# Sink-window attention with a squared-ReLU expert layer: shorter first legs for chunks 0 and 1, and another order of their attention

## The chip, the cores and the metric

One Trainium2 chip, one of its cores. The metric is the device time of one execution in microseconds. The engines of the core are TensorE (PE; its weight loads are listed as PEld), VectorE (DVE), ScalarE (ACT), GpSimd (POOL) and SyncE (SP), which issues nearly all DMAs. Each engine runs its instructions in the order in which they stand, and waits where the next one lacks its data.

## What is computed

```python
# q, k, v: (4, 8, 768, 64); n_sink 4, window 128
scores = q @ k.T / 8
keep = is_sink | in_window          # the first 4 keys, and the 128 keys up to the query
a = softmax(where(keep, scores, -1e9))      # sums get 1e-9 added
x = (a @ v)                         # heads side by side: (3072, 512)
h = maximum(x @ w_in, 0)            # w_in (512, 2048)
out = (h * h) @ w_out               # w_out (2048, 512)
```

## The kernel before

The 3072 rows of x are worked in eight chunks of 384 rows (two for each batch). A chunk has four pairs of heads and three blocks of 128 queries. Attention of one pair goes through these steps: `score` (TensorE multiplies q by the keys of the block, VectorE masks and finds the row's maximum, ScalarE takes the exponential and its sum); `normalise` (VectorE's reciprocals, then GpSimd scales the probabilities P, three pieces for each head, and copies the sink columns to PSK); `probs` (TensorE transposes P, ScalarE or VectorE copies the result to PTF); `sink_keys` (the same for the sink columns); and `values` (TensorE multiplies by v into xo, ScalarE writes the upper part of x, VectorE the rest, xl). For chunks 0 and 1 `probs` and `sink_keys` stand together in `tail`, a generator of three steps.

The expert layer runs over 16 blocks of 128 hidden columns. For one block TensorE does twelve matmuls of 384 columns (ph, from x and w_in), ScalarE takes the ReLU r and its square gh, VectorE the rest of the square gl, and then TensorE adds nine matmuls of 512 columns into three accumulators po (from gh, gl and w_out). A block is four steps of the generator `moe`, here called quarter steps. The matmuls use fp32r in two parts, upper and rest, so each weight row is split into two parts first.

The weights come as 32 rows of 512 KB: four of w_in and four of w_out for each quarter of the hidden columns, in this order. `split_steps` splits one row in five steps on VectorE (lines 561 to 574) and two copies on ScalarE (lines 560 and 573). The tile m between them has a single buffer. A row is loaded when the one two places ahead of it has been split.

A leg is a chunk's pass over a part of the hidden blocks. Where a chunk has more than one leg, `evacuate` stores the accumulators po to DRAM (part), and the next leg's `evacuate` loads them and VectorE adds them (line 518). Chunks 0 and 1 go in legs of one half, chunk 0, 1, 0, 1, so that their first legs need only half of the rows. The other six chunks have one leg each.

Up to the end of chunk 1's attention the order on all engines is written out by hand (`tc.manual_schedule`): the loop from line 653 on runs chunk 0's attention and the scores of chunk 1's first pair (pair 4), and `fill(n)` puts n steps of row splitting between. Then the list `todo` has the rest of chunk 1's attention in small items, and after every quarter step of chunk 0's first leg some steps of splitting and one item of `todo` follow. QUANTA is the number of these quarter steps, EARLY the number of rows split by then. Behind that, a plan (line 757) gives for each leg up to which of the attention units of later chunks it goes (`ready[1]` is 0, `ready[2]` the end of chunk 2's units), between which rows it splits, and how fast; the scheduler orders the engines by priority there.

Scores in `todo` go into two banks (tag att), and so do the transposed probabilities; in the loop ahead of it scores also use the banks h, o0 and o1, which the expert layer needs later. Ahead of that, matmuls on zeros (`busy`) fill TensorE while the first pair is prepared.

Of the kernel before, what the change touches and what calls it, by code (L numbers as in the profile page):

```python
# [8 lines left out]
F32 = mybir.dt.float32  # L9
# [9 lines left out]
P = 128  # L19
# [22 lines left out]
def sink_window_attention_moe(  # L42
# [25 lines left out]
    with ExitStack() as fast:  # L68
# [206 lines left out]
        def normalise(c, p, heads):  # L275
# [10 lines left out]
            for hh in heads:  # L286
                Pt = st["P"][hh]
                j0 = 1 if half == 0 else 0
                if c > 1:

                    nc.gpsimd.tensor_tensor(  # L291
                        Pt[:, j0:NQ, 0:P], Pt[:, j0:NQ, 0:P], Pt[:, j0:NQ, BS:BAND], op=ALU.add
                    )
                for j in range(NQ):
                    n = P if j < j0 else (BS if c > 1 else BAND)
                    nc.gpsimd.tensor_scalar(  # L296
                        Pt[:, j, 0:n], Pt[:, j, 0:n], rs[:, hh, j : j + 1], 1.0, op0=ALU.mult, op1=ALU.mult
                    )
                own = slice(hh * NS, hh * NS + NS)
                src = Pt[:, i0:NQ, P:BS]  # L300
                to = PSK[p % 2 if c < 2 else 0].rearrange("p q (t c) -> p q t c", c=2 * NS)[:, 0 : NQ - i0]
                nc.gpsimd.tensor_copy(to[:, :, 0:3:2, own], src.unsqueeze(2).broadcast_to([P, NQ - i0, 2, NS]))
                nc.gpsimd.tensor_tensor(to[:, :, 1, own], src, f32(to[:, :, 0, own]), op=ALU.subtract)
# [201 lines left out]

        def evacuate(c, f0, f1, po):
            for t in range(NQ):
                pool, tag = (ap3, "PTF") if c == NCHUNK - 1 and t == 2 else (mp, "ob")
                ob = pool.tile([P, DM], F32, tag=tag, name=f"ob_{c}_{f0}_{t}")
                r0 = c * TOK + t * P  # L510
                if c == NCHUNK - 1 and t == NQ - 1:
# [9 lines left out]
                else:  # L521
                    nc.vector.tensor_copy(ob, po[t])  # L522
                if f1 < NFC:
                    part[c, t] = dp.tile([P, DM], F32, tag=f"part{c}{t}", name=f"part_{c}_{t}")
                    nc.sync.dma_start(out=part[c, t], in_=ob)
                else:
                    nc.sync.dma_start(out=out[r0 : r0 + P, :], in_=ob)
# [77 lines left out]
                split.append(n)  # L605
                yield

        FH = NFC // 2
        legs = [(0, 0, FH), (1, 0, FH), (0, FH, NFC), (1, FH, NFC)] + [(c, 0, NFC) for c in range(2, NCHUNK)]
        products = moe(legs)  # L610
        QUANTA = 4 * FH
        EARLY = HALF + 2
        with tc.manual_schedule(engines={E.PE, E.DVE, E.Activation, E.Pool, E.SP}):
            steps = row_steps()

# [34 lines left out]
            split_sinks = load_sinks(0)  # L650
            busy(7)

            for s in range(NPAIR + 1):
                if s > 0:
                    load_qk(*pairs[s + 1])
                for i, tags in enumerate((("att", "att"), ("h", "h"), ("o0", "o1"))):
                    scores(s, i, tags)
                    fill(1)
                fill(1)

                normalise(*pairs[s], (0, 1))
# [5 lines left out]
                if s > 0:  # L667
# [5 lines left out]
                    if rest:  # L673
                        rest()
                    next(t)
                    fill(1)
                    next(t)
                else:
                    fill(1)
            rest = values(*pairs[NPAIR - 1], True)  # L680
            fill(2)
            rest()

            todo = []
            for s in range(NPAIR + 1, 2 * NPAIR + 1):
                if s < 2 * NPAIR:
                    todo += [lambda s=s: (s + 1 < 2 * NPAIR and load_qk(*pairs[s + 1]), scores(s, 0))]
# [10 lines left out]
            todo.append(lambda: values(*pairs[2 * NPAIR - 1]))  # L698
            for n in range(QUANTA):
                next(products)  # L700
                fill(2 if n < QUANTA // 2 and n % 3 or n % 4 == 0 or n >= QUANTA - 12 else 1)
                if todo:
                    todo.pop(0)()
            while len(split) < EARLY:
# [49 lines left out]

        LEAD = 2.5

        plan = [(ready[1], EARLY, 27, 1.0), (ready[1] + 24, 27, NROW, 0.7), (ready[2], NROW, NROW, 1.0)]
        plan += [(ready[min(c + 1, NCHUNK - 1)], NROW, NROW, 1.0) for c in range(2, NCHUNK)]
        flag = None
        checked = 0  # L760
# [219 lines left out]
```

## Time and profile before

| | us |
|---|---|
| median of three runs | 709.92 (709.29 to 710.59) |
| the profiled execution | 708.76 |
| its span, first to last instruction | 706.7 |
| TensorE busy | 687.6 |
| VectorE busy | 437.6 |
| ScalarE busy | 428.7 |
| GpSimd busy | 230.2 |

The busy times are of the whole span. Matmuls are pipelined, so the duration of one overlaps with the next; the distance from start to start is the shorter time.

### The profile page before, as it was taken

To read this page: it belongs to the slowest core of one execution; us is meant where nothing else is said; L and a number is where in the kernel's file an instruction comes from. 1 tells how busy PE (TensorE), PEld (TensorE's weight loads), DVE (VectorE), ACT (ScalarE), POOL (GpSimd) and SP (SyncE) were. 2 spreads that over 40 slices of the span, in tenths; PEclk is the share of its full clock that TensorE was granted. 3 is DMA by queue.
4 is the path that set the end of the run, shared out by engine and by line. 5 is a ranking of instruction groups with operands and counts; after the bars stand their busy time and mean duration, and the time that the engine had idled before them with its cause. 6 is when DMAs were issued, how large, how long until landed. Compare 5 with 4: busy or idle time off the path is not lost.

```text
span 706.7 us, 11716 instructions
## 1 busy us (share of the span) xinstructions
PE 687.6 (97%) x3866; PEld 593.9 (84%) x3866; DVE 437.6 (62%) x1183; ACT 428.7 (61%) x1200; POOL 230.2 (33%) x436
## 2 busy tenths in 40 slices
PE   8789999999999999999999999999999999999996
PEld 4557788998888888888888888889888898889995
DVE  8998889945657655565656565665555655542231
ACT  5887777755666766766676676667767454422221
POOL 6645400043455424323433443332344233200000
PEclk9999999999999999999999999999999999999998
DMA  8475457421534433333343532344333310000001
GB/s 262 144 233 169 129 163 233 142 74 42 149 65 120 131 107 94 85 108 107 94 112 104 150 90 80 95 128 115 98 88 84 96 44 15 1 11 36 1 0 50
DMA packets 37028, 71.51 MB, mean 101 GB/s; under 512 B 4384, under 2 KB 14368, under 8 KB 36960
## 3 DMA queue, kind: packets, MB, share of 16 engines
q1 hardware_dynamic: 36816, 70.55, 34.1%
q8 instruction: 33, 0.54, 0.3%
q14 instruction: 35, 0.29, 0.1%
q10 hardware_dynamic: 144, 0.13, 0.1%
HBM read 62.80 MB, written 7.86 MB: 100 GB/s over the span
## 4 chain that ended last, share of the span: by engine, by line
PE 86%; ACT 5%; DVE 3%; DMA 3%; issue 1%; SPq 0%; ACTq 0%; DVEq 0%
PE po L494 35%; PE ph L457 35%; PE xo L398 6%; PE s L264 4%; PE pt L368 2%; ACT P L271 2%; PE xo L401 2%; DMA kn<-in_k_dram 1%; PE s L260 1%; PE pt L350 1%; ACT m L560 1%; DVE P L268 1%; DMA part<-ob 1%; PE pss L310 1%; DMA raw<-in_moe_w_in_dram 1%
## 5 line engine op out<-in xcount | busy, mean ns | idle before, releaser
L457 PE MATMUL ph<-x,wi 128*128 128x384 f32 x1536 | 305.8, 340 | 0.0
L457 PEld LDWEIGHTS ph<-x,wi 128*128 128x128 f32 x1536 | 265.0, 188 | 8.8 <-issue 1.4
L494 PE MATMUL po<-wo,gh 128*128 128x512 f32 (+1 forms) x770 | 244.3, 398 | 1.1 <-DVE ob L522 0.6
L232 POOL TENSOR_TENSOR KS<-kn,KS 128x408 fp32r<-128x408 f32 (+1 forms) x48 | 58.5, 1218 | 318.9 <-ACT KS L231 315.1
L494 PEld LDWEIGHTS po<-wo,gh 128*128 128x128 f32 x770 | 135.8, 188 | 19.9 <-issue 1.4
L494 PE MATMUL po<-wo,gl 128*128 128x512 f32 x385 | 151.6, 394 | 0.0
L271 ACT ACTIVATE P<-P,nbs 128x264 f32<-128x264 f32 (+1 forms) x192 | 94.4, 492 | 75.5 <-DVE nbs L268 75.1
L465 ACT ACTIVATE r<-ph 128x384 f32<-128x384 f32 x128 | 62.3, 486 | 91.8 <-PE ph L457 89.2
L475 DVE TENSOR_TENSOR ph<-ph,r 128x384 f32<-128x384 f32 x104 | 58.4, 562 | 72.6 <-ACT r L465 72.5
L268 DVE CUSTOM_DVE_ANT_0 P<-s,masks 128x264 f32<-128x264 f32 x160 | 67.1, 429 | 57.2 <-PE s L264 53.8
L296 POOL TENSOR_SCALAR P<-P,rs 128x136 f32<-128x136 f32 (+2 forms) x192 | 85.4, 460 | 34.6 <-DVE rs L285 17.8
L494 PEld LDWEIGHTS po<-wo,gl 128*128 128x128 f32 x385 | 72.2, 188 | 16.0
L479 DVE TENSOR_TENSOR gl<-ph,gh 128x384 fp32r<-128x384 f32 x128 | 71.1, 556 | 23.3 <-ACT ph L472 12.8
L468 ACT ACTIVATE gh<-r 128x384 fp32r<-128x384 f32 x128 | 67.2, 525 | 3.0
L234 DVE TENSOR_TENSOR QS<-qn,QS 64x384 fp32r<-64x384 f32 x48 | 47.3, 984 | 26.5 <-ACT QS L233 26.1
L291 POOL TENSOR_TENSOR P<-P 128x256 f32<-128x256 f32 (+1 forms) x48 | 50.4, 1050 | 24.1 <-ACT P L271 23.6
L264 PE MATMUL s<-KS,QS 128*128 128x264 f32 (+1 forms) x288 | 57.4, 281 | 0.3 <-DVE nbs L268 0.3
L264 PEld LDWEIGHTS s<-KS,QS 128*128 128x128 f32 x288 | 52.0, 188 | 5.6 <-DVE nbs L268 1.2
L374 DVE TENSOR_TENSOR PTF<-pt,halves 128x256 f32<-128x256 f32 x96 | 36.3, 419 | 22.3 <-PE pt L368 21.7
L398 PE MATMUL xo<-PTF,vn 128*64 128x256 f32 (+1 forms) x448 | 47.4, 348 | 2.5 <-ACT PTF L357 2.5
L398 PEld LDWEIGHTS xo<-PTF,vn 128*64 128x64 f32 x448 | 31.7, 138 | 19.8 <-issue 10.1
L231 ACT CAST KS<-kn 128x408 fp32r<-128x408 f32 (+1 forms) x48 | 28.2, 588 | 32.5 <-issue 18.9
(104 smaller groups left out, 632.4 us busy)
## 6 DMA issues: line engine op xcount, KB each, us to landing
raw<-in_moe_w_in_dram SPq DMA_DIRECT2D x16, 512.0 KB, 4.5
raw<-in_moe_w_out_dram SPq DMA_DIRECT2D x16, 512.0 KB, 3.5
half<-in_moe_w_in_dram SPq DMA_DIRECT2D x32, 256.0 KB, 3.2
half<-in_moe_w_out_dram SPq DMA_DIRECT2D x32, 256.0 KB, 3.0
kn<-in_k_dram SPq DMA_DIRECT2D x24, 272.0 KB, 4.2
qn<-in_q_dram SPq DMA_DIRECT2D x32, 192.0 KB, 3.7
out_dram<-ob SPq DMA_DIRECT2D x23, 256.0 KB, 2.3
kn<-in_k_dram SPq DMA_DIRECT2D x24, 204.0 KB, 3.6
```

Of the source, the lines that this page charges most:

```text
L232: nc.gpsimd.tensor_tensor(KS[:, 1, 0:nk], st["kn"][:, hh, 0:nk], f32(KS[:, 0, 0:nk]), op=ALU.subtract)
L264: nc.tensor.matmul(ps[:, 0:n], st["QS", hh][:, qcols], flat[:, a, c0 : c0 + n], start=(a == 0), stop=(a == 1))
L268: nc.vector.tensor_tensor_reduce(Pt[:, i, 0:n], ps[:, 0:n], mask[:, 0:n], -SCALE, BIG, ALU.add, ALU.min, nb)
L271: nc.scalar.activation(Pt[:, i, 0:n], Pt[:, i, 0:n], AF.Exp, bias=nb, scale=-1.0, accum_out=sm[:, i : i + 1])
L296: nc.gpsimd.tensor_scalar(Pt[:, j, 0:n], Pt[:, j, 0:n], rs[:, hh, j : j + 1], 1.0, op0=ALU.mult, op1=ALU.mult)
L398: nc.tensor.matmul(xo[h * D : h * D + D, cols], lhsT, rhs, start=(n == 0), stop=False, skip_group_check=True)
L457: nc.tensor.matmul(ph[:, 0:TOK], wi_at(i, cc, fc), xt[:, cc, :], start=(m == 0), stop=(m == 3 * NCC - 1),)
L465: nc.scalar.activation(r, ph[:, 0:TOK], AF.Relu)
L468: nc.scalar.activation(gh, r, AF.Square)
L475: nc.vector.tensor_tensor(ph[:, 0:TOK], ph[:, 0:TOK], r, op=ALU.mult)
L479: late = lambda: nc.vector.tensor_tensor(gl, ph[:, 0:TOK], f32(gh), op=ALU.subtract)
L494: nc.tensor.matmul(po[t][:, e], gt[:, ts_], wo[f][:, i, e], start=(f == f0 and j == 0), stop=(f == f1 - 1 and j == 2), skip_group_check=True,)
```

## The change

There are now three cuts of the hidden blocks for chunks 0 and 1: a quarter, a quarter and a half, chunk 0 and 1 in turn, so six legs instead of four. The first leg has 16 quarter steps instead of 32, EARLY is 9 rows instead of 18, and after each quarter step an item of `todo` comes ahead of the splitting steps (one or two of them) and another behind. In chunk 0's loop most splitting steps between scores go away, except for pair 0. Of pair 4's three groups of scores only the first stands ahead of chunk 0's last values; the other two are the first items of `todo`. Pair 3's second head is scaled by ScalarE instead of GpSimd. The sums of the second quarter leg use the three PTF buffers instead of the two ob buffers, and line 470's `spare` (not changed) now holds for the four blocks of chunk 0's second quarter, whose squares go to ScalarE.

```diff
@@ normalise
                     n = P if j < j0 else (BS if c > 1 else BAND)
+                    if (c, p, hh) == (0, NPAIR - 1, 1):
+                        nc.scalar.activation(Pt[:, j, 0:n], Pt[:, j, 0:n], AF.Copy, scale=rs[:, hh, j : j + 1])
+                        continue
                     nc.gpsimd.tensor_scalar(
@@ evacuate
-                pool, tag = (ap3, "PTF") if c == NCHUNK - 1 and t == 2 else (mp, "ob")
+                pool, tag = (ap3, "PTF") if c == NCHUNK - 1 and t == 2 or f0 == NFC // 4 else (mp, "ob")
...
-        FH = NFC // 2
-        legs = [(0, 0, FH), (1, 0, FH), (0, FH, NFC), (1, FH, NFC)] + [(c, 0, NFC) for c in range(2, NCHUNK)]
+        FQ, FH = NFC // 4, NFC // 2
+        cuts = ((0, FQ), (FQ, FH), (FH, NFC))
+        legs = [(c, f0, f1) for f0, f1 in cuts for c in range(2)] + [(c, 0, NFC) for c in range(2, NCHUNK)]
         products = moe(legs)
-        QUANTA = 4 * FH
-        EARLY = HALF + 2
+        QUANTA = 4 * FQ
+        EARLY = NCC + 5
...
-            for s in range(NPAIR + 1):
+            for s in range(NPAIR):
                 if s > 0:
                     load_qk(*pairs[s + 1])
+                ahead = s == 0
                 for i, tags in enumerate((("att", "att"), ("h", "h"), ("o0", "o1"))):
                     scores(s, i, tags)
-                    fill(1)
+                    if ahead or i == NQ - 1:
+                        fill(1)
                 fill(1)
...
                     next(t)
-                    fill(1)
                     next(t)
                 else:
                     fill(1)
+            load_qk(*pairs[NPAIR + 1])
+            scores(NPAIR, 0)
+            fill(1)
+            rest = values(*pairs[NPAIR - 2], True)
+            load_v(*pairs[NPAIR])
+            t = tail(NPAIR - 1, ("o2", "h"))
+            next(t)
+            fill(1)
+            rest()
+            next(t)
+            fill(2)
+            next(t)
+            fill(1)
             rest = values(*pairs[NPAIR - 1], True)
-            fill(2)
+            fill(3)
             rest()
-            todo = []
+            todo = [lambda i=i: scores(NPAIR, i) for i in range(1, NQ)] + [lambda: normalise(*pairs[NPAIR], (0, 1))]
...
                 next(products)
-                fill(2 if n < QUANTA // 2 and n % 3 or n % 4 == 0 or n >= QUANTA - 12 else 1)
+                if todo:
+                    todo.pop(0)()
+                fill(1 + n % 2)
                 if todo:
                     todo.pop(0)()
...
-        plan = [(ready[1], EARLY, 27, 1.0), (ready[1] + 24, 27, NROW, 0.7), (ready[2], NROW, NROW, 1.0)]
+        plan = [(ready[1], EARLY, 14, 1.0), (ready[1], 14, 18, 1.0), (ready[1], 18, 23, 1.0)]
+        plan += [(ready[1] + 10, 23, NROW, 0.8), (ready[2], NROW, NROW, 1.0)]
```

In the rows that follow, a name ends with the number of its buffer; s and P carry pair and head ahead of it (s also the block of queries), ph the hidden block, po the first block of its leg and the accumulator. The chunk is not printed.

On VectorE, the scores of pair 2, before:

```order
L268 ISA P_2_1_362,nbs<-s_2_1_0_363,mask_117 128x128
L268 ISA nbs 128x1
L563 SCALAR_TENSOR_TENSOR t_2_339<-raw_177,t_2_339 128x512
L268 ISA P_2_0_357,nbs<-s_2_0_1_368,masks 128x264
L268 ISA nbs 128x1
L268 ISA P_2_1_362,nbs<-s_2_1_1_372,masks 128x264
L268 ISA nbs 128x1
L565 TENSOR_SCALAR m_340<-raw_177 128x512
L268 ISA P_2_0_357,nbs<-s_2_0_2_377,masks 128x264
```

and now:

```order
L268 ISA P_2_1_352,nbs<-s_2_1_0_353,mask_117 128x128
L268 ISA nbs 128x1
L268 ISA P_2_0_347,nbs<-s_2_0_1_357,masks 128x264
L268 ISA nbs 128x1
L268 ISA P_2_1_352,nbs<-s_2_1_1_361,masks 128x264
L268 ISA nbs 128x1
L268 ISA P_2_0_347,nbs<-s_2_0_2_365,masks 128x264
```

The steps of row 2 between the three groups are gone; the row is split later.

On TensorE, from chunk 0's last transposes to the first matmuls of the expert layer, before, all three score groups of pair 4 stand ahead of pair 2's and pair 3's values:

```order
L260 MATMUL s_0_0_0_546<-kn_0_447,qn_0_446 128x264
L260 MATMUL s_0_1_0_551<-kn_0_447,qn_0_446 128x264
L260 MATMUL s_0_0_1_556<-kn_0_447,qn_0_446 128x264
L260 MATMUL s_0_1_1_560<-kn_0_447,qn_0_446 128x264
L260 MATMUL s_0_0_2_569<-kn_0_447,qn_0_446 128x264
L260 MATMUL s_0_1_2_573<-kn_0_447,qn_0_446 128x264
L398 MATMUL xo_2_596<-PTF_2_2_537,vn_2_414 64x256
```

and now, the first group alone:

```order
L353 MATMUL pt_2_2_509<-ident,P_2_1_352 128x128 x4
L260 MATMUL s_0_0_0_523<-kn_0_434,qn_0_433 128x264
L260 MATMUL s_0_1_0_528<-kn_0_434,qn_0_433 128x264
L401 MATMUL xo_2_536<-PTF_2_2_514,vn_2_402 64x256
L401 MATMUL xo_2_536<-PTF_2_1_507,vn_2_402 64x128
```

Four of the six score rows have moved behind chunk 0's last values and the first matmuls of ph_0.

On TensorE, the stretch in which pair 5 (pair 1 of chunk 1) begins, now:

```order
L460 MATMUL ph_0_599<-x_0_400,wi 128x384
L260 MATMUL s_1_0_0_660<-kn_1_517,qn_1_516 128x264
L260 MATMUL s_1_1_0_665<-kn_1_517,qn_1_516 128x264
L260 MATMUL s_1_0_1_670<-kn_1_517,qn_1_516 128x264
L260 MATMUL s_1_1_1_674<-kn_1_517,qn_1_516 128x264
L260 MATMUL s_1_0_2_683<-kn_1_517,qn_1_516 128x264
L260 MATMUL s_1_1_2_687<-kn_1_517,qn_1_516 128x264
L353 MATMUL pt_0_0_707<-ident,P_0_0_522 128x128 x4
L460 MATMUL ph_1_714<-x_0_399,wi 128x384 x2
```

where before it stood like this:

```order
L260 MATMUL s_1_1_0_674<-kn_1_540,qn_1_539 128x264
L457 MATMUL ph_0_653<-x_0_411,wi 128x384 x2
L457 MATMUL ph_0_653<-x_0_412,wi 128x384
L457 MATMUL ph_0_653<-x_0_411,wi 128x384 x2
L457 MATMUL ph_0_653<-x_0_412,wi 128x384
L260 MATMUL s_1_0_1_695<-kn_1_540,qn_1_539 128x264
```

Half a block of the expert layer stood between pair 5's first two groups of scores, and stands there no more.

## Rows read from the trace of the kernel before

**Rows 1.** The page: the span, and TensorE's busy time, share and instructions.
```profile
span 706.7 us, 11716 instructions
...
PE 687.6 (97%) x3866; PEld 593.9 (84%) x3866; DVE 437.6 (62%) x1183; ACT 428.7 (61%) x1200; POOL 230.2 (33%) x436
```

**Rows 2.** Stretches: length; PE, PEld, DVE, ACT, POOL busy; granted clock; DMA share; GB/s.
```profile
17.20:24.60 7.40, 6.10 (x37) 4.46 (x36) 6.75 (x26) 5.80 (x18) 4.84 (x11) 0.77 0.24 77
...
31.60:41.10 9.50, 7.02 (x50) 4.60 (x51) 9.05 (x31) 6.09 (x18) 5.79 (x15) 1.00 0.72 238
41.10:61.10 20.00, 19.03 (x99) 13.60 (x98) 18.34 (x55) 17.21 (x46) 8.45 (x14) 1.00 0.57 186
...
103.60:134.30 30.70, 30.07 (x151) 26.92 (x150) 29.35 (x66) 24.36 (x46) 0.00 (x0) 1.00 0.60 193
```

**Rows 3.** Waits of TensorE, 11 to 41 us: total, times, longest.
```profile
PE s L260 <- ACT PTF L357: 3.7, 3, 1.8
PE xo L398 <- ACT PTF L357: 2.5, 1, 2.5
```

**Rows 4.** TensorE in order of time: start, duration, instruction, idle before it.
```profile
18.93 1.38 PE L260 MATMUL s<-kn,qn 64*128 64x128 f32 x10 [1.30 <-ACT PTF L357]
20.24 2.27 PE L398 MATMUL xo<-PTF,vn 128*64 128x256 f32 x12
...
25.72 1.38 PE L260 MATMUL s<-kn,qn 64*128 64x128 f32 x10 [0.62 <-ACT PTF L357]
27.03 1.30 PE L398 MATMUL xo<-PTF,vn 128*64 128x256 f32 x12
...
31.60 2.21 PE L260 MATMUL s<-kn,qn 64*128 64x264 f32 x12 [1.76 <-ACT PTF L357]
...
39.04 1.88 PE L398 MATMUL xo<-PTF,vn 128*64 128x256 f32 x12 [2.48 <-ACT PTF L357]
...
41.08 1.21 PE L457 MATMUL ph<-x,wi 128*128 128x384 f32 x6
...
96.27 0.44 PE L401 MATMUL xo<-SK,VS 128*128 128x384 f32 x1
```

**Rows 5.** VectorE in order of time, one step and the same place five later.
```profile
125.12 0.69 DVE L563 SCALAR_TENSOR_TENSOR t<-raw,t 128x512 int32<-128x512 int32 x1
...
127.34 0.55 DVE L479 TENSOR_TENSOR gl<-ph,gh 128x384 fp32r<-128x384 f32 x1
```

**Rows 6.** Groups by line, 0 to 110 us: busy, mean ns, idle before.
```profile
L271 ACT ACTIVATE P<-P,nbs 128x264 f32<-128x264 f32 x40 | 20.2, 506 | 5.3 <-DVE nbs L268 5.1
...
L560 ACT COPY m<-raw 128x512 uint16<-128x512 uint16 x22 | 17.0, 772 | 3.1 <-issue 1.4 <-DVE wi L574 1.1 <-DVE wo L574 0.4
```

**Rows 7.** GpSimd in order of time, the first and the last instruction of pair 4.
```profile
37.67 1.40 POOL L296 TENSOR_SCALAR P<-P,rs 128x264 f32<-128x264 f32 x3 [3.26 <-DVE rs L285]
...
42.29 0.75 POOL L303 TENSOR_TENSOR PSK<-P,PSK 128x24 fp32r<-128x24 f32 x1
```

**Rows 8.** TensorE in order of time, a score group of chunk 1.
```profile
42.21 0.72 PE L260 MATMUL s<-kn,qn 64*128 64x264 f32 x4
```

**Rows 9.** The chain that ended last, around 115 us: start, us, what.
```profile
114.83 2.08 PE ph L457 x12
116.91 2.06 PE po L494 x9
```

**Rows 10.** VectorE and TensorE in order of time, at two ends of legs.
```profile
109.28 0.69 DVE L522 COPY ob<-po 128x512 f32<-128x512 f32 x1 [1.11 <-DMA part<-ob]
...
110.03 0.73 PE L494 MATMUL po<-wo,gh 128*128 128x512 f32 x2 [0.63 <-DVE ob L522]
...
182.85 0.73 PE L494 MATMUL po<-wo,gh 128*128 128x512 f32 x2 [0.47 <-DVE ob L518]
```

**Rows 11.** Stretches, as in rows 2.
```profile
21.00:22.00 1.00, 1.00 (x8) 0.62 (x5) 1.00 (x6) 1.00 (x4) 0.63 (x2) 0.50 0.00 0
...
36.00:40.00 4.00, 1.52 (x13) 0.89 (x12) 3.59 (x13) 2.99 (x9) 2.18 (x6) 1.00 0.99 326
```

## What I predict

> **What bounds the kernel now.** I read the page first: TensorE is busy for 687.6 of 706.7 us [rows 1]. So only three things can shorten the kernel: TensorE standing still, TensorE at the lower clock, or TensorE running pieces slowly. The end of the program, the last leg and its stores, is not touched. The stretch table then shows where the stops are [rows 2]: from 31.6 to 41.1 us TensorE works 7.02 of 9.50 us, while VectorE works 9.05. From 103.6 to 134.3 us VectorE works 29.35 of 30.70 us, yet TensorE only stops for 0.63. The waits of TensorE between 11 and 41 us name ScalarE's copy of the transposed probabilities, 3.7 us before scores and 2.5 us before values [rows 3]. In order of time these are the stops before 18.93, 25.72, 31.60 and 39.04 us, and the first matmul of the expert layer starts at 41.08 us [rows 4]. That copy is late because ScalarE and VectorE run in order, and between two attention steps each does a step of a weight row.
>
> **The change, part by part.** Everything is counted as TensorE time lost or won.
>
> *Fewer row steps ahead of the first expert matmul.* Before, 31 steps of weight splitting stand ahead of it (5 for pair 0, then four times 6, then 2); after, 22 (5, then three times 3, then 8). Five VectorE steps of one row take 125.12 to 127.34 us, so 0.44 us each from start to start [rows 5]. Pairs 1 to 3 lose three steps each, 1.3 us of VectorE, and 0.6 of a row's two ScalarE operations, the one of 772 ns [rows 6] and one somewhat shorter. I walked the new order from 11.4 us on, up to where it equals the old one, with the durations of these rows. Scores of pair 2 resume at 17.8 instead of 18.93 us, since the copy no longer stands behind row work; pair 3's at 23.6 instead of 25.72; pair 4's at 29.1 instead of 31.60.
>
> *The second head of pair 3 on ScalarE.* GpSimd ends a later pair 5.4 us after its start (37.67 to 43.04) [rows 7]. The trace has no such scaling on ScalarE. Its nearest row is the exponential with the same shape, 506 ns [rows 6]; three take 1.3 us from start to start if they need no accumulator read. They run beside GpSimd's first head, and hold ScalarE's next copies for that long. Bounds: from a loss of 1.3 us, if those copies are what is waited for, to a gain of 1.4 us, if GpSimd is. In my walk both end within 0.5 us of each other, so I count a gain of 0.4 us, already in the times below.
>
> *Values before scores.* With two of pair 4's three score groups moved behind, values of pair 3 start at 34.1 instead of 39.04 us and the first expert matmul at 35.6 instead of 41.08 us [rows 4]. **Term 1: -5.5 us**, bounds -7.0 (VectorE's whole saving of nine steps, 4.0, and the reads of the moved scores and ScalarE's exponentials for them, 3.0) and -3.5 (three periods of 1.3 less a delay of 0.4 by ScalarE's scaling).
>
> *The moved scores* are still to be done: two groups of four matmuls at 0.72 us [rows 8]. **Term 2: +1.4 us.**
>
> *Chunk 1's attention in 16 quarter steps instead of 32.* From 41.08 until its last values end (96.5 us) before, 55.5 us pass. They hold 30.5 us of expert work, counted at 2.08 us for twelve matmuls of the first layer and 2.06 for nine of the second [rows 9]. So attention, with its waits and the changes between kinds of matmul, takes 25.0 us. After, 17.4 us of expert work stands beside it. If attention costs what it did, its end comes at 35.6 + 1.4 + 25.0 + 17.4 = 79.4 us; the old kernel has the same work done at 83.4 us. But there is less to hide the waits with. I walked the densest place, the middle of pair 4 to the second half of the second hidden block: pair 5's three score groups stand in a row. They share two banks, so each waits until VectorE has read the one before, and VectorE first ends a row (0.44 us a step) and waits for pair 4's exponentials, 0.5 us each on ScalarE. The transposes then wait for GpSimd, which starts pair 4 only at 40.2 us and needs 5.4 us [rows 7]. I get 12.5 us for 8.7 us of work: 3.8 us lost. Behind it two items per quarter step keep TensorE nearly full, and ten changes of kind fewer (46 against 56) give back about 1 us. All in all I count 7.1 us lost, against 6.7 before in the same count. **Term 3: +0.4 us**, bounds -1.0 (only the fewer changes count) and +4.0 (each of the three later pairs loses half of what this one does, on top of the former loss).
>
> *Two more seams.* A seam is where a leg's three output accumulators are emptied before the next leg may fill them. Before, one copying seam cost 0.63 us, where VectorE waited 1.11 us for an output buffer's store; one adding seam cost 0.47 us [rows 10]. After, the quarter legs add an adding seam for each chunk; the sums use three other buffers, so no store is waited for there. The adds stand among row steps, but twelve matmuls of the next block (2.08 us) run over them: three adds of 0.6 us just fit, and their loads were issued a leg earlier. **Term 4: +0.3 us**, bounds 0 and +2.5. The squares of four blocks move from VectorE to ScalarE at the same time; ScalarE has room (24.36 of 30.70 us [rows 2]).
>
> *Chunk 2's attention.* Only 10 instead of 24 of its units fall in the leg before last, so 44 fall in the last one of chunk 1. Counted like ScalarE's work below, VectorE has some 34 us there beside 54 us of TensorE. **Term 5: +0.4 us**, bounds 0 and +2.0 for longer waits of its transposes.
>
> Sum: -5.5 + 1.4 + 0.4 + 0.3 + 0.4 = **-3.0 us**. The profiled execution took 708.76 us, 1.16 below the median of the runs shown, 709.92. So 705.8 for an execution like the profiled one, and **706.9 us** as a median.
>
> **The clock.** From 17.2 to 24.6 us the granted clock is 0.77 on average [rows 2], and in 21 to 22 it stands at 0.50, the lower of its two levels; ahead of it TensorE had stood still for 1.30 us. Values that take 1.30 us at 27.03 take 2.27 us at 20.24 [rows 4]. Worked out from the mean, 7.4 us x 0.23 are lost, 1.7 us. Yet in 36 to 40 us TensorE worked only 1.52 of 4 us at a clock of 1.00 [rows 11]. I leave the clock out of the sum. The Trainium skill (TensorE: Matmul & The Clock Gate, What's actually happening) says that the low clock is the default and that activity lifts it. By that rule the dense stretch, with its many short stops, would fall to the lower level again, and the sum would be -1.3 with one fall and +0.4 with two.
>
> **The rivals.** *Head wins fully, nothing is given back:* terms 1 to 3 at -7.0 + 1.4 - 1.0, the last two at 0: 703.3 us. For it: GpSimd and ScalarE have slack in the head. Against it: the two banks. *The dense stretch eats the gain:* term 3 at +3.5 us gives 710.0 us, no change. For it: the new order's ScalarE instructions there, at their durations from start to start, make some 36 us beside 40 us of TensorE. Against it: between 41 and 61 us ScalarE was as full, 17.21 of 20 us [rows 2], and TensorE lost only 1 us. *The clock falls* once or twice in that stretch, by the mechanism above: 708.6 to 710.3 us. *Slower: VectorE lags at the seams.* In the second quarter leg of chunk 1 I count 18.0 us of VectorE against 16.6 of TensorE. If its lag is not worked off there, each of the two new adding seams finds its adds behind a row's 2.2 us: 1.8 + 2.2 - 2.08 = 1.9 us each. With a second copying seam's 0.63 and the lag of 1.4 that makes 5.8 us in the place of term 4, so 712.4 us. The sign turns from 0.7 us a seam on, with the other two. Against it: 29.35 of 30.70 us of VectorE, from 103.6 on, cost TensorE no more than the 0.63.
>
> **How the numbers follow.** Forecast 0.40, full win 0.17, dense stretch 0.18, clock 0.08, seams 0.17. A difference below 0.2% (1.4 us) is about what a measurement of this kernel can't tell from none. Faster holds the first two and a part of the clock: 0.60. Slower holds the seams and the bad end of the dense stretch: 0.21. Same: 0.19. The range reaches to the full win and, of the seams, to their cheaper half: 703.3 to 711.0 us. The likeliest case alone spans 704.5 to 708.3.
>
> **What would show it.** First expert matmul at 35.6 us (33.5 to 37.5). TensorE's waits between 36 and 48 us on VectorE's score reads and ScalarE's copies, some 4 us. Chunk 1's last values at 79.5 us (76 to 83). Waits before the second layer behind an add, under 0.5 us each. The granted clock at 1.00 in 36 to 48 us. Span 703.7 us. I am wrong if the first expert matmul is not earlier than 38 us, if the stretch to 80 us loses more than 10 us, or if TensorE stops more than 1.5 us at a seam.

## The result, and the profile after

The changed kernel takes 715.44 us (median of four runs, 714.03 to 717.03) against 709.61 for the kernel before: ratio 1.0078, 95% interval 1.0064 to 1.0091. It is slower by 5.8 us where I forecast 3 us less, and lies outside the range. The profiled execution took 714.03 us. Two executions of this document's runs that show a mean clock of 0.75 (one of e14) and 0.82 (one of the kernel before) are left out of every median and ratio.

The page after (to compare with [rows 1]): TensorE is busy 2.6 us longer, and idle for 3.0 us more.

```profile
span 712.3 us, 11772 instructions
...
PE 690.2 (97%) x3865; PEld 594.7 (83%) x3866; DVE 436.3 (61%) x1185; ACT 431.2 (61%) x1207; POOL 221.1 (31%) x433
```

TensorE after, in order of time (start, duration, instruction, idle before it; compare [rows 4, 8]):

```profile
29.97 1.40 PE L260 MATMUL s<-kn,qn 64*128 64x264 f32 x4 [1.97 <-ACT PTF L360]
31.30 2.40 PE L401 MATMUL xo<-PTF,vn 128*64 128x256 f32 x12
...
36.56 1.30 PE L401 MATMUL xo<-PTF,vn 128*64 128x256 f32 x12 [1.07 <-ACT PTF L360]
...
38.02 1.20 PE L460 MATMUL ph<-x,wi 128*128 128x384 f32 x6
39.15 0.72 PE L260 MATMUL s<-kn,qn 64*128 64x264 f32 x4
40.40 1.06 PE L260 MATMUL s<-kn,qn 64*128 64x264 f32 x4 [0.53 <-DVE nbs L268]
...
44.78 1.06 PE L260 MATMUL s<-kn,qn 64*128 64x264 f32 x4 [1.43 <-DVE nbs L268]
46.03 1.06 PE L260 MATMUL s<-kn,qn 64*128 64x264 f32 x4 [0.18 <-DVE nbs L268]
47.36 0.63 PE L353 MATMUL pt<-ident,P 128*128 128x128 f32 x4 [0.27 <-DVE nbs L268]
...
84.86 0.44 PE L404 MATMUL xo<-SK,VS 128*128 128x384 f32 x1
```

The first expert matmul starts at 38.02 us, 3.1 earlier than before and not 5.5. Then come stops where the scores of pairs 4 and 5 wait for VectorE. A group of four score matmuls takes 1.06 us behind such a stop, 0.72 otherwise, since its second head waits for VectorE's read of its own bank, which starts 0.35 us after the first head's (at 40.61 and 40.26 us for the group at 40.40).

TensorE's waits after, 38 to 86 us (total, times, longest), 4.0 us in all:

```profile
PE s L260 <- DVE nbs L268: 3.2, 5, 1.4
PE pt L353 <- ACT PTF L360: 0.5, 1, 0.5
PE pt L353 <- DVE nbs L268: 0.3, 1, 0.3
```

and before, 41 to 97 us, 1.9 us:

```profile
PE pt L350 <- ACT PTF L357: 0.8, 1, 0.8
PE s L260 <- DVE nbs L268: 0.8, 1, 0.8
PE pt L350 <- ACT SK L317: 0.3, 1, 0.3
```

ScalarE and GpSimd after, in order of time:

```profile
27.86 1.21 ACT L297 ACTIVATE P<-P,rs 128x128 f32<-128x128 f32 x3 [0.53 <-DVE rs L285]
...
29.34 1.07 ACT L360 COPY PTF<-pt 128x512 f32<-128x512 f32 x2
```

```profile
30.06 0.22 POOL L306 TENSOR_TENSOR PSK<-P,PSK 128x16 fp32r<-128x16 f32 x1
43.36 1.83 POOL L299 TENSOR_SCALAR P<-P,rs 128x264 f32<-128x264 f32 x3 [13.07 <-PE s L260]
...
47.80 0.24 POOL L306 TENSOR_TENSOR PSK<-P,PSK 128x24 fp32r<-128x24 f32 x1
```

ScalarE's three scalings wait for VectorE's reciprocals and then take 1.21 us; behind them stand the copies for which TensorE waits 1.97 us ahead of 29.97. GpSimd stands still for 13 us and starts on pair 4 at 43.36, against 37.67 before [rows 7] and 40.2 in my walk.

Stretches after (columns as in [rows 2]):

```profile
31.00:34.00 3.00, 3.00 (x14) 1.79 (x14) 1.72 (x6) 1.73 (x5) 0.00 (x0) 0.50 0.26 103
36.00:40.00 4.00, 3.30 (x23) 2.25 (x23) 3.85 (x9) 2.18 (x5) 0.00 (x0) 1.00 0.64 246
...
110.00:140.00 30.00, 30.00 (x154) 27.32 (x152) 29.59 (x65) 21.36 (x42) 0.00 (x0) 1.00 0.77 264
150.00:170.00 20.00, 20.00 (x106) 18.27 (x105) 5.26 (x13) 7.87 (x22) 3.57 (x7) 1.00 0.08 24
170.00:232.00 62.00, 59.63 (x359) 50.05 (x357) 42.93 (x137) 41.40 (x124) 36.00 (x65) 1.00 0.43 114
```

The clock falls once, as before, but at another place: values take 2.40 us at 31.30 for it. VectorE is full from 110 to 140 us and TensorE doesn't mind, nearly idle from 150 to 170, and from 170 on, where chunk 2's attention is crowded, TensorE stands still for 2.37 us (1.01 in 170.00 to 227.60 before).

TensorE at the ends of legs and in chunk 2's attention (compare [rows 10]). The two stops at ends of legs are at seams that the kernel before has too (0.63 and 0.47 us there); at the two new adding seams, around 122 and 138 us, TensorE has no stop above 0.15 us:

```profile
107.92 0.74 PE L497 MATMUL po<-wo,gh 128*128 128x512 f32 x2 [0.43 <-DVE ob L526]
...
181.53 0.73 PE L497 MATMUL po<-wo,gh 128*128 128x512 f32 x2 [0.75 <-DVE ob L522]
...
223.12 0.52 PE L264 MATMUL s<-KS,QS 128*128 128x264 f32 x2 [1.13 <-DVE nbs L268]
```

**Where the time went.** I compare at places where the same attention is done, and take off the expert matmuls done by then at the prices of [rows 9]. *A* is the time from the first expert matmul to the end of chunk 1's last values (85.30 us after, 96.71 before), less these, and less 1.4 us where two of pair 4's score groups fall into it. Before it is 96.71 - 41.08 = 55.63, less 97 and 60 matmuls of the two layers (16.8 and 13.7): 25.1 us. After it is 47.28 - 9.9 (57) - 7.6 (33) - 1.4 = 28.4. *B* is counted in the same way from there to the end of the values of chunk 3's first pair, where both kernels have done 408 and 294 expert matmuls (at 227.91 and 232.37 us): 23.7 before, 26.5 after. So -3.1 at the first expert matmul, +1.4 for the moved scores, +3.3 in A and +2.8 in B: 4.4 us, and the last matmul ends 4.46 us later too (704.11 against 699.65). The sum is one profile of each kernel. What follows the last matmul took 1.2 us longer in this execution than before; in the later profiles it takes 6.5 to 7.7 us, before 7.0, here 8.2, so I put that down to this execution.

### The profile page after: what moved, and what is told of

The parts are those of the page before. It is cut to its first block, busy times and chain, and to the rows that moved or that the text cites. A ratio compares the mean times of both kernels' runs of the same rounds, so it can differ in the third digit from the quotient of the medians.

```text
span 712.3 us, 11772 instructions
## 1 busy us (share of the span) xinstructions
PE 690.2 (97%) x3865; PEld 594.7 (83%) x3866; DVE 436.3 (61%) x1185; ACT 431.2 (61%) x1207; POOL 221.1 (31%) x433
## 4 chain that ended last, share of the span: by engine, by line
PE 86%; ACT 5%; DVE 3%; DMA 3%; issue 1%; POOL 1%; SPq 0%; ACTq 0%; DVEq 0%; POOLq 0%
PE ph L460 35%; PE po L497 35%; PE xo L401 5%; PE s L264 4%; PE pt L371 2%; ACT P L271 2%; PE xo L404 1%; PE s L260 1%; DVE P L268 1%; PE pt L353 1%; POOL P L299 1%; DMA kn<-in_k_dram 1%; ACT m L564 1%; DMA raw<-in_moe_w_in_dram 1%; PE pss L313 1%
## 5 line engine op out<-in xcount | busy, mean ns | idle before, releaser
L478 DVE TENSOR_TENSOR ph<-ph,r 128x384 f32<-128x384 f32 x100 | 56.2, 562 | 74.1 <-ACT r L468 73.8
L299 POOL TENSOR_SCALAR P<-P,rs 128x128 f32<-128x128 f32 (+2 forms) x189 | 80.3, 440 | 35.5 <-DVE rs L285 13.2
L482 DVE TENSOR_TENSOR gl<-ph,gh 128x384 fp32r<-128x384 f32 x128 | 71.2, 556 | 24.6 <-ACT ph L475 13.7
L234 DVE TENSOR_TENSOR QS<-qn,QS 64x384 fp32r<-64x384 f32 x48 | 46.0, 958 | 26.9 <-ACT QS L233 26.5
L401 PE MATMUL xo<-PTF,vn 128*64 128x256 f32 x448 | 47.0, 348 | 1.1 <-ACT PTF L360 1.1
L401 PEld LDWEIGHTS xo<-PTF,vn 128*64 128x64 f32 x448 | 31.8, 138 | 18.3 <-issue 9.5
L231 ACT CAST KS<-kn 128x408 fp32r<-128x408 f32 (+1 forms) x48 | 28.2, 588 | 27.8 <-issue 15.8
```

Source lines behind the costliest of these rows:

```text
L299: nc.gpsimd.tensor_scalar(Pt[:, j, 0:n], Pt[:, j, 0:n], rs[:, hh, j : j + 1], 1.0, op0=ALU.mult, op1=ALU.mult)
L401: nc.tensor.matmul(xo[h * D : h * D + D, cols], lhsT, rhs, start=(n == 0), stop=False, skip_group_check=True)
L478: nc.vector.tensor_tensor(ph[:, 0:TOK], ph[:, 0:TOK], r, op=ALU.mult)
L482: late = lambda: nc.vector.tensor_tensor(gl, ph[:, 0:TOK], f32(gh), op=ALU.subtract)
```

## The experiments

Ratios are to the kernel before on the same chip, with their 95% interval; A and B as above, from one profile each; "falls" counts the low stretches of the granted clock between 13 and 60 us in it.

| kernel | us | ratio | first expert matmul | A | B | falls |
|---|---|---|---|---|---|---|
| before | 709.61 | 1 | 41.08 | 25.1 | 23.7 | 1 |
| changed | 715.44 | 1.0078 (1.0064 to 1.0091) | 38.02 | 28.4 | 26.5 | 1 |
| e1 head alone | 713.46 | 1.0054 (1.0041 to 1.0068) | 36.63 | 31.8 | 23.3 | 3 |
| e2 legs alone | 713.91 | 1.0051 (1.0037 to 1.0064) | 41.31 | 28.6 | 26.7 | 2 |
| e3 GpSimd scales | 712.82 | 1.0044 (1.0028 to 1.0061) | 35.68 | 29.7 | 27.0 | 1 |
| e4 24 units | 711.66 | 1.0027 (1.0015 to 1.0040) | 36.69 | 30.0 | 24.9 | 1 |
| e5 = e3 and e4 | 710.10 | 0.9998 (0.9988 to 1.0008) | 35.87 | 29.7 | 24.4 | 1 |
| e6 = e5, zeros in stops | 709.33 | 0.9984 (0.9972 to 0.9995) | 35.72 | 28.4 | 24.2 | 0 |
| e7 = e5, other banks | 709.16 | 0.9980 (0.9970 to 0.9990) | 35.52 | 28.2 | 24.5 | 1 |
| e8 old legs, new head | 710.66 | 1.0003 (0.9993 to 1.0013) | 36.56 | 32.3 | 23.6 | 2 |
| e9 = e5, scores ahead | 710.72 | 1.0008 (0.9996 to 1.0019) | 37.58 | 30.5 | 25.2 | 2 |
| e10 = e5, rows later | 710.06 | 0.9992 (0.9980 to 1.0004) | 35.65 | 30.2 | 24.8 | 1 |
| e11 changed, zeros in stops | 714.02 | 1.0053 (1.0035 to 1.0072) | 37.61 | 28.5 | 26.8 | 0 |
| e12 = e7, zeros in stops | 709.22 | 0.9989 (0.9980 to 0.9999) | 35.49 | 28.0 | 24.7 | 0 |
| e13 legs alone, zeros | 714.84 | 1.0061 (1.0042 to 1.0081) | 42.39 | 27.5 | 25.2 | 1 |
| e14 before, zeros | 711.72 | 1.0022 (1.0009 to 1.0035) | 42.78 | 25.1 | 23.3 | 1 |

**The two halves.** e1 has the new loop of chunk 0 with the old legs and plan, e2 the old loop with the new legs and plan.

```diff
 e1
+        legs = [(0, 0, FH), (1, 0, FH), (0, FH, NFC), (1, FH, NFC)] + [(c, 0, NFC) for c in range(2, NCHUNK)]
...
-                if todo:
-                    todo.pop(0)()
-                fill(1 + n % 2)
+                fill(3 if n < QUANTA // 2 and n % 3 == 0 else 2)
```

> The changed kernel's loop of chunk 0 (fewer row steps, values of pair 3 ahead of two of pair 4's score groups, ScalarE scaling pair 3's second head), but with the legs, the plan and the one item of todo per quarter step of the kernel before; row steps behind each quarter step are raised to two or three, so that the weights still come in time. Theory A, the legs spend the gain: in the changed kernel's trace the first expert matmul starts 3.1 us earlier, and 1.4 us of scores are still to be done, so about 1.6 us are kept, 3.3 if the granted clock does not fall to 0.50 in the loop: 706.3 to 708.0 us against 709.6. Theory B, the order of the head is itself what opens the stops between 38 and 48 us (pair 4's scores and normalising come late whatever legs follow): the 2.7 us lost there stay, and the time is 709.5 to 711 us.

> The kernel before up to chunk 0's last values (31 row steps, all of pair 4's scores ahead, GpSimd scaling), then the six legs, the new plan, the two items of todo per quarter step and the other buffers for the quarter legs' sums. Theory A, the legs spend the gain: chunk 1's attention is squeezed and costs some 2 us in stops, the seams and chunk 2's attention 2.7 us: 713 to 715 us, about as slow as the changed kernel or 1 to 2 us better. Theory B, the stops come from the head's order: only the 2.7 us of the later part remain, 711.5 to 712.5 us, and chunk 1's last values end before 88 us.

Each half alone is slower than the kernel before, by 3.8 and 3.6 us by the ratios. e1 keeps its early start (36.63 us) and loses 6.7 us in A. Two stretches of its profile:

```profile
42.70:45.90 3.20, 3.20 (x10) 2.27 (x8) 2.70 (x8) 2.02 (x6) 1.06 (x2) 0.50 0.89 233
...
53.00:100.00 47.00, 45.91 (x270) 36.25 (x270) 44.40 (x107) 37.18 (x87) 21.23 (x32) 1.00 0.56 175
```

and one of the kernel before:

```profile
57.00:104.00 47.00, 45.93 (x279) 37.07 (x278) 40.07 (x95) 35.23 (x80) 15.20 (x22) 1.00 0.49 153
```

With legs of a half the row steps taken out ahead of the first expert matmul come back right behind it: VectorE works 44.40 us there against 40.07 before. But TensorE stands still for 1.09 us in this stretch, as before (1.07), so it isn't shown that these row steps are what A loses. Two of the three falls of the clock lie in A, worth up to 1.3 us each (below), and the stops before scores make 2.8 us in three, against 0.8 before. B's direction holds, and its time is passed by 2.5 us. For e2 theory A's time holds, and A and B are near those of the changed kernel; in part that is luck, since e2's A has a fall of the clock in it, and the changed kernel's has not (e13, with the same legs and no fall there, has 27.5 us).

**Two parts undone.** e3 removes the three lines of ScalarE's scaling, e4 changes one number, e5 does both.

```diff
-        plan += [(ready[1] + 10, 23, NROW, 0.8), (ready[2], NROW, NROW, 1.0)]
+        plan += [(ready[1] + 24, 23, NROW, 0.8), (ready[2], NROW, NROW, 1.0)]
```

> The changed kernel with the scaling of pair 3's second head back on GpSimd. Theory A, ScalarE's scaling shortens the way to the first expert matmul by 0.4 to 1.4 us: then this one's first expert matmul comes that much later than 38.0 us and GpSimd's start on pair 4 too, and the time is 716 to 717.5 us against 715.4. Theory B, ScalarE's copies are what is waited for there (1.07 us before the values at 36.56): the first expert matmul comes up to 1 us earlier and the time is 714 to 715 us.

> The changed kernel with 24 instead of 10 of chunk 2's units planned into the leg before last of chunk 1 and 0. Theory A, the 2.7 us lost between 85 and 232 us come from crowding chunk 2's attention into one leg: 1 to 2 us come back, 713.5 to 714.5 us. Theory B, VectorE has no room in the leg before (29.59 of 30 us between 110 and 140) and the attention units there wait or push the row splitting: no gain or a loss, 715 to 718 us.

> The changed kernel with two parts undone: pair 3's second head scaled by GpSimd (alone 712.8 us against 715.4 for the changed kernel) and 24 of chunk 2's units in the leg before last (alone 711.7). Theory A, both losses stand apart, 1.0 us before the first expert matmul and 1.5 us between 170 and 232 us, and the rest of what the two showed is the granted clock, which falls more or less often from run to run: 709.8 to 711 us. Theory B, the two together overfill GpSimd's or VectorE's room and the gains don't add: 711.5 us or more.

Theory B of e3 holds, and the gain is larger than said: with GpSimd the first expert matmul comes earlier. e5's ScalarE and TensorE:

```profile
27.84 1.06 ACT L357 COPY PTF<-pt 128x512 f32<-128x512 f32 x2
```

```profile
28.47 1.19 PE L260 MATMUL s<-kn,qn 64*128 64x264 f32 x4 [0.23 <-ACT PTF L357]
...
32.76 0.33 PE L310 MATMUL pss<-ident,PSK 128*128 128x128 f32 x1 [0.91 <-POOL PSK L303]
...
34.41 1.30 PE L398 MATMUL xo<-PTF,vn 128*64 128x256 f32 x12 [0.68 <-ACT PTF L357]
...
35.87 1.20 PE L457 MATMUL ph<-x,wi 128*128 128x384 f32 x6
42.63 1.06 PE L260 MATMUL s<-kn,qn 64*128 64x264 f32 x4 [1.42 <-DVE nbs L268]
```

The copies start at 27.84 instead of 29.34 us and the stop of 1.97 us is 0.23. GpSimd is now waited for, 0.91 us, so not all of it is kept. e4, which still scales on ScalarE, shows the price with no fall of the clock until then:

```profile
30.20 1.20 PE L260 MATMUL s<-kn,qn 64*128 64x264 f32 x4 [1.97 <-ACT PTF L360]
31.33 1.30 PE L401 MATMUL xo<-PTF,vn 128*64 128x256 f32 x12
...
36.69 1.22 PE L460 MATMUL ph<-x,wi 128*128 128x384 f32 x6
```

36.69 - 35.87 = 0.8 us for the scaling on ScalarE, and 38.02 - 36.69 = 1.3 us for the fall at 31 us in the changed kernel's profile, with the same code ahead of it. For e4 theory A holds and more: B is 24.2 to 25.2 us in all kernels with 24 units and six legs, 26.5 to 27.0 with 10, 23.3 to 23.7 with four legs. In the stretch that stood nearly idle, VectorE now works 11.69 us instead of 5.26:

```profile
150.00:170.00 20.00, 19.73 (x106) 17.81 (x106) 11.69 (x35) 13.12 (x36) 8.65 (x15) 1.00 0.22 58
```

So in B the plan's number costs 2 us and the two more legs, with their order of rows, about 1. Of the 2 us some 1.1 is the stop at 223.12 us, which e4 and e5 don't have.

e5 is as fast as the kernel before, and the gains add: by the ratios e3 wins 2.4 us on the changed kernel, e4 3.6, and e5 5.7. That is the whole loss. The profiled executions differ by less, 1.5, 2.2 and 4.2 us, and where the rest lies they don't show; the executions of one kernel differ in their mean clock (0.991 to 0.994 in the changed kernel's, 0.992 to 0.999 in e5's).

**The clock.** e6 and e11 put matmuls on zeros into TensorE's stops: ahead of pair 4's first scores, of pair 3's values and of pair 5's second score group.

```diff
+            busy(5, "o0")
             scores(NPAIR, 0)
...
+            busy(3, "o0")
             rest = values(*pairs[NPAIR - 1], True)
...
+                    todo += [lambda s=s, i=i: ((s, i) == (NPAIR + 1, 1) and busy(5, "o0"), scores(s, i)) for i in range(1, NQ)]
```

> The kernel of the run before in this set, with 13 matmuls on zeros put into TensorE's stops: five ahead of pair 4's first scores, three ahead of pair 3's values, five ahead of pair 5's second score group (stops of 1.97, 1.07 and 1.43 us in the changed kernel's trace). Theory A, falls of the granted clock, seen in every profile so far at a different place between 20 and 53 us, cost 1.3 to 1.7 us each and come from TensorE's stops: no fall is seen, the spread of the runs narrows, and the time is 1.3 to 2.5 us under that of the kernel without them, 707.5 to 709.5 us. Theory B, the falls don't follow from these stops, or the added matmuls are in the way: a fall is still seen, and the time is the same or up to 1.5 us more.

> The changed kernel with nothing undone, and the 13 matmuls on zeros of the earlier set in TensorE's stops at 28, 35.5 and 43.4 us. There they took the mean clock to 0.998 and gave 0.8 us. Theory A, of the changed kernel's 5.8 us the granted clock makes 1.3 to 3 (its runs have clocks of 0.991 to 0.994): 712.4 to 714 us and clocks of 0.996 or more in most runs. Theory B, the clock is no part of it, since low stretches fall together with stops that would be there anyway: 714.5 to 716 us.

e6 shows no fall from 5.3 us on:

```profile
5.30:60.00 54.70, 47.62 (x297) 31.36 (x299) 45.60 (x162) 41.70 (x125) 30.82 (x73) 1.00 0.63 193
```

Its A is 28.4 us, e5's with a fall inside is 29.7: such a fall costs 1.3 us. The medians gain 0.8 us (e5 to e6) and 1.4 (changed to e11), though in both cases the intervals of the ratios overlap: less than theory A's lower bound in e6, inside its range in e11, and e11 is still slower than before by 0.53%. The clock is at most a part of the loss. The Trainium skill (TensorE: Matmul & The Clock Gate, What's actually happening) says that activity lifts the clock from a low default; that e6, e11 and e12 show no fall agrees with it.

The profiled executions of e6 and e11 are no faster than those of e5 and the changed kernel (710.05 against 709.79 us, 714.25 against 714.03). Behind B they have a stop that the others lack, at the end of chunk 1's last leg, where VectorE waits for the stored sums to be loaded. e6's TensorE and VectorE:

```profile
230.58 0.73 PE L494 MATMUL po<-wo,gh 128*128 128x512 f32 x2 [1.18 <-DVE ob L519]
```

```profile
229.84 0.69 DVE L519 TENSOR_TENSOR ob<-po,ob 128x512 f32<-128x512 f32 x1 [1.34 <-DMA ob<-part]
```

In e11 the stop is 0.87 us, in e13 1.34; the other nine profiles with six legs and the four with four legs don't have it. So that load's lateness is one more difference of about 1 us between executions.

**What makes A longer.** e7 takes other banks for three score groups, e9 undoes the move of pair 4's scores, e10 moves row steps, e8 tries the old legs with e7's banks and zeros in the loop.

```diff
 e7
+            FREE = {(NPAIR, 1): ("o0", "o1"), (NPAIR + 1, 0): ("o0", "o1"), (NPAIR + 1, 2): ("o2", "xo")}
 e9
-            scores(NPAIR, 0)
+            for i, tags in enumerate((("att", "att"), ("h", "h"), ("o0", "o1"))):
+                scores(NPAIR, i, tags)
             fill(1)
+            normalise(*pairs[NPAIR], (0, 1))
 e10
-                fill(1 + n % 2)
+                fill(0 if n < 4 else 2)
```

> The first kernel of this set with three of the five score groups at the start of chunk 0's first leg in other banks (o0, o1, o2, xo, which are free until the first output matmul): the two moved groups of pair 4 and pair 5's three then no longer share two banks. Theory A, the shared banks make the stops of 0.53, 1.43, 0.18 and 0.27 us there, as in the prediction: they shrink to under 1 us in sum, and the time is 1 to 1.5 us under the first kernel's. Theory B, VectorE's reads, ScalarE's exponentials and GpSimd's late scaling are what the pairs wait for, so the stops only move to the transposes: same time within 0.5 us.

> The legs, plan and single todo items of the kernel before, with the changed loop of chunk 0 (GpSimd scaling), the other banks of the run before in this set, and eight matmuls on zeros in the stops ahead of pair 4's scores and pair 3's values. If the new order of chunk 0's loop is worth its 4 to 5 us and only banks, clock and legs gave them back: 706 to 708 us, faster than the kernel before. If the gain is given back wherever chunk 1's attention follows, because VectorE has as many row steps and scores to do by then: 709 to 711 us.

> The kernel with the two parts undone (GpSimd scaling, 24 units; 710.1 us, first expert matmul at 35.87 us, four stops of 2.4 us in sum between 38 and 46 us) and one part more: all three of pair 4's score groups and its normalising stand ahead of chunk 0's last values again. Theory A, the stops come from the move: GpSimd starts on pair 4 at 41.20 us there, against 37.67 in the kernel before, and the pairs behind queue up. Then GpSimd starts before 38 us, the stops shrink to under 1 us, the first expert matmul comes 1.5 to 2 us later and the time is 708.5 to 709.5 us. Theory B, the scores ahead hold ScalarE's copies as in the kernel before (a stop of 2.48 us before its last values): the first expert matmul comes after 38.5 us, and the time is 710 to 711.5 us.

> The same kernel of 710.1 us, but with no row steps behind the first four quarter steps and two behind each later one (six steps of 0.44 us each on VectorE, and their ScalarE copies, go out of the stretch from 38 to 46 us). Theory A, VectorE is what the scores wait for there, because row steps stand between its reads: the stops of 2.4 us shrink to about 1 us, pair 4 reaches GpSimd 1 us earlier, and the time is 708.3 to 709.5 us. Theory B, the chain of score read, exponential, sum and GpSimd's 5.4 us of pair 4 sets the pace: the stops stay within 0.5 us and the time within 0.6 us of 710.1.

e7's TensorE has one stop where there were four:

```profile
38.99 1.60 PE L260 MATMUL s<-kn,qn 64*128 64x264 f32 x12
43.34 1.09 PE L350 MATMUL pt<-ident,P 128*128 128x128 f32 x4 [2.75 <-DVE nbs L268]
```

The stop is as long as the four (2.4 us in e5), as theory B said. It ends when VectorE has read pair 5's second score group (from 42.77 to 43.20 us), whose banks the transposes take. What the other banks give is the restarts, groups at 0.72 us or less instead of 1.06. Against e5 that is 0.9 us in the median, less than theory A's and more than theory B's; e12 and e6, both without a fall, differ by 0.4 in A. In e9 GpSimd starts pair 4 at 33.85 us, but then ScalarE's six exponentials for pair 4 (until 33.23 us) and two pieces of row splitting, 0.60 and 0.77 us, stand ahead of the copies for pair 3's values, so the stop stands there. e9's GpSimd, ScalarE and TensorE:

```profile
33.85 1.41 POOL L296 TENSOR_SCALAR P<-P,rs 128x264 f32<-128x264 f32 x3 [1.91 <-ACT wi L574]
```

```profile
33.13 0.60 ACT L574 CAST wi<-t 128x512 fp32r<-128x512 f32 x1
...
34.01 0.58 ACT L357 COPY PTF<-pt 128x512 f32<-128x512 f32 x1
34.49 0.77 ACT L561 COPY m<-raw 128x512 uint16<-128x512 uint16 x1
35.12 0.57 ACT L357 COPY PTF<-pt 128x512 f32<-128x512 f32 x1
```

```profile
35.74 1.53 PE L398 MATMUL xo<-PTF,vn 128*64 128x256 f32 x12 [2.04 <-ACT PTF L357]
```

By this run the move shifts a stop rather than makes one; theory B's time is right, though its late start (after 38.5 us) is not. In e10 the stops before scores are 2.3 us in five instead of e5's 3.2 in five, so the row steps are a part of them and not the whole; 1.1 us are lost again where weights come late, and the time stays. e8, with other banks and zeros, loses more in A than e1 (32.3 us against 31.8), in three stops of 1.4 to 2.8 us; its time is that of its second case.

**Squeeze or move.** e13 and e14 hold zeros in the old loop's stops; they differ in legs, plan, todo and the splitting steps between its items alone. e12 adds zeros to e7.

```diff
+                    if (s, i) in ((2, 1), (NPAIR, 0)):
+                        busy(3 if s == 2 else 5, "o0")
                     scores(s, i, tags)
...
+            busy(8, "o0")
             rest = values(*pairs[NPAIR - 1], True)
```

> The kernel with GpSimd scaling, 24 units and three score groups in other banks (709.16 us against 710.37 for the kernel before), and 13 matmuls on zeros in its stops: five ahead of pair 4's first scores, three ahead of pair 3's values, five ahead of pair 4's first transposes, where it stood still for 2.75 us. If the gain of the clock (0.8 us in the earlier set) and that of the banks (0.9) add: a ratio to the kernel before of 0.9965 to 0.9975, some 708 us. If the two cured the same stops: 0.998, some 709.

> The six legs alone, behind the unchanged loop of chunk 0, with 24 units for chunk 2, and matmuls on zeros in the stops of that loop (three ahead of pair 2's second score group, five ahead of pair 4's scores, eight ahead of pair 3's values). Against the next kernel, which has the same matmuls and the old legs, this is what 16 instead of 32 quarter steps for chunk 1's attention, and the seams, cost by themselves. Theory A, the squeeze alone makes most of the 3.3 us that the changed kernel loses between its first expert matmul and chunk 1's last values: 2.5 to 4 us slower than the next kernel. Theory B, the move of pair 4's scores makes most of it: 0 to 1.5 us slower.

> The kernel before, with the matmuls on zeros of the run before in this set and nothing else. If the one fall of the clock in its profile (20.4 to 23.8 us) costs 1 to 1.7 us, it is 0.5 to 1.5 us faster than the kernel before; if the fall lies beside stops that are there anyway, it is the same within 0.5 us.

A is 27.5 us in e13 and 25.1 in e14, and neither has a fall in it: the squeeze into 16 quarter steps costs 2.4 us alone, with chunk 0's row steps and pair 4's scores where they were. The medians differ by 3.1, inside theory A's range, but that holds the later legs too (B is 25.2 against 23.3); the squeeze itself is read from A, one profile of each. The largest waits of e13 and e14, 42 to 98 us (with the smaller ones 4.2 against 2.0 us until chunk 1's last values), show where:

```profile
PE s L260 <- DVE nbs L268: 1.8, 3, 0.6
PE pt L350 <- ACT PTF L357: 1.1, 2, 0.7
PE pt L350 <- DVE nbs L268: 0.6, 1, 0.6
```

```profile
PE pt L350 <- ACT PTF L357: 0.9, 2, 0.8
PE s L260 <- DVE nbs L268: 0.8, 1, 0.8
```

The remaining 0.9 of the 3.3 us is then the new loop's, by subtraction. That is not shown: the parts don't simply add, since e1, the new loop without the squeeze, loses 6.7 us in A, some 4 of them without its two falls. How the new loop loses that much beside the old legs stays open. e14 itself is slower than the kernel before: its first matmuls on zeros came behind the stop of 1.30 us that they were to fill, which lies inside a score group, so they lay on the path and the clock fell all the same. e12 ends at e7's time, as its second case said: the gains of banks and zeros don't add. e7 is the best version, 0.2% under the kernel before (0.1 to 0.3), about the least that can be told from no change.

## Why the prediction was wrong

No single step sets the sign: with any one of the three mis-sized terms as forecast the sum of the four measured parts stays above zero (+1.5 us with term 3, +2.0 with term 1, +2.3 with terms 4 and 5). Term 3 was off by most, 2.9 us; term 1 was off by 2.4, terms 4 and 5 by 2.1.

- **Term 1**, -5.5 us, measured -3.1. The walk to the first expert matmul was nearly right without the scaling: 35.6 said with a gain of 0.4 for it, so 36.0 without, and 35.7 to 35.9 in e3, e5 and e6. I counted ScalarE's scaling as that gain; it costs 0.8 by the profiles, inside the bound of 1.3 that I had named for it, and 2.1 to 2.4 by the ratios of e5 to e4 and of e3 to the changed kernel. The fall of the clock, left out of the sum, took 1.3 more.
- **Term 2**, +1.4, stands: eight matmuls at the old price.
- **Term 3** is the step that failed by most: +0.4 us, measured +3.3. I let attention cost what it did, found 3.8 us lost in the first dense place, and then let two items per quarter step and fewer changes of kind pay it back. But attention costs more TensorE time when fewer expert matmuls stand between its steps: 4.0 us of stops instead of 1.9, and four more score groups that restart at 1.06 instead of 0.72 us (1.4). The squeeze alone makes 2.4 (e13 against e14); the rest is not settled. With other banks the stop only moved, to transposes that wait for VectorE's read of the scores in theirs, so what was late was VectorE. The rival with +3.5 us had the size of this term; it named ScalarE's fullness, where 3.2 of the 4.0 us wait for VectorE's reads of the scores, and its time, 710.0 us, was too low by the other terms.
- **Terms 4 and 5**, +0.7, measured +2.8. Two more legs cost about 1 us instead of 0.3, but not by stops at seams: those are 0.43 and 0.75 us here, 0.63 and 0.47 before, and the new adding seams have none above 0.15. So the seam rival fell. Ten instead of 24 units cost 2.0, my upper bound: I compared VectorE's sum with TensorE's over the leg, but the attention of chunk 2 lost by its density, while VectorE idled in the leg ahead of it (5.26 of 20 us).
- **The clock** stayed at 1.00 in 36 to 48 us in this profile and fell at 31, so the rival's place was wrong in this execution; in e3, e4, e5, e7 and e10 it fell between 42 and 50, in the dense stretch. The median is 1.4 us above the profiled execution, and its other runs have a mean clock of 0.991 to 0.992 against 0.994.

Term by term: -3.1 + 1.4 + 3.3 + 2.8 = +4.4 us, 1.2 after the last matmul, so 5.6 in all, and 708.76 + 5.6 gives 714.4 against 714.03 measured. What is left open: what the 1 us of the two more legs is, how the loss in A splits between the squeeze and the new loop, and where the ratios of e3, e4 and e5 win what their profiles don't show.

## What to carry to other kernels

Moving a start forward is worth only what the work behind it can spare as cover: here attention hid its waits behind expert matmuls, and with half the cover it cost 2.4 us more (e13 against e14), where the earlier start gave 3.1. Where a chain runs over three engines, price the density (stops and slow restarts), not each engine's busy sum. Before work is handed to an engine with room, look at what stands next in its queue: 1.21 us of scaling ahead of two copies made a stop of 0.23 us into 1.97.

## What I had not expected of the hardware

The same code had its falls of the granted clock at other places from run to run (at 31 us in the changed kernel, at 46 in e4, with the same code up to there), each worth up to 1.3 us, and mean clocks between 0.991 and 0.998 for the kernel before, one of 0.943 aside. Matmuls on zeros in front of the stops went with a clock that stayed up: 13 of them took the mean to 0.998 in e6's profile. In e14 the first three came behind their stop, the clock fell there all the same, the mean was 0.995, and the first expert matmul came 1.7 us later than before.
